# A column order and an operand place of its own for each Strassen tile (f32 attention and gated feed-forward, one core)

## The chip, the cores and the metric

The kernel runs on one core of a Trainium2 chip. The metric is the time of one execution on the device in microseconds (us). A core has TensorE for matrix products (PE in the profile; PEld is its loading of weights), VectorE (DVE), ScalarE (ACT), GpSimd (POOL), and SyncE (SP), which here issues all DMAs. SBUF is the on-chip memory, 128 partitions wide; PSUM holds the results of products. In a matmul one operand, the weights, is loaded into TensorE first, and the columns of the other, the moving operand, run through it.

## The reference

```python
def _attn_ref(q, k, v, g_norm):                       # 8 batches, 8 heads, 576 tokens, 64
    kv = np.einsum('bhsd,bhse->bhde', k, v)
    out = np.einsum('bhsd,bhde->bhse', q, kv)
    rms = np.sqrt(np.mean(out * out, axis=-1, keepdims=True) + 1e-06)
    return out / rms * g_norm

def _moe_ref(x, w_in, w_out):                         # x 4608 x 512, w_in 512 x 2048, w_out 2048 x 512
    h = x @ w_in
    g = h * (1.0 / (1.0 + np.exp(-h)))
    return g @ w_out
```

The output of the attention, with the heads of a token side by side, is the x of the second function. All is f32.

## The kernel before

**Precision.** Each f32 operand of the large products is split into an upper part that TensorE's faster f32 format (fp32r) holds exactly and a lower part, the rest. One product becomes three matmuls: upper by lower, lower by upper, upper by upper.

**Tiles.** The 4608 tokens are nine tiles of 512, t = 0 to 8. Tiles 0 and 1 form h = x @ w_in plainly: for each of the 16 blocks of 128 hidden units, `products` (line 470) issues 12 matmuls of 512 columns (line 474). Tiles 2 to 8 are the Strassen tiles: w_in and x are cut into quarters, and seven half-sized products on sums of quarters replace eight. Their sums of w_in are made during tile 1 (`make_sums`), sent to DRAM and loaded again for each step.

**A pair step** (`pair_step`, line 649) does a lower and an upper block of a Strassen tile, i = 0 to 7. It issues the products 1, 2, 6, 7, then 4, 5, 3, six matmuls each (`product`, line 628): 42 matmuls of 256 columns on line 634, whose weights are parts of w_in and whose moving operand is one of x's seven operands. Between them stand the projections of earlier blocks (`project`, line 499; line 505): gated h as weights, a block of w_out moving, 512 columns, three matmuls for each of four groups of 128 tokens and each of two blocks, 24 in a step. In the last tile one of the four groups is done in two halves of 256 columns. VectorE and ScalarE combine the products and apply the gate. The attention of later batches (lines 253 to 318) is spread over the steps of tiles 2 to 6 by a plan written out by hand; each engine runs its queue in the order of the code.

**x's operands.** `make_operand` (line 622) splits one of the seven sums of x into upper (ACT, line 625) and lower (DVE, line 626) parts of 256 columns by two row blocks: 4096 bytes a partition. This happens once a tile: `prepare` in the last step of the tile before makes 1, 2, 6, 7 when those products have been issued, and 4, 5, 3 after theirs. The dictionary `seven` gives each product its home j: 0 to 3 are inside x_place, the tile that held x of tile 1 (`x_second`), 4 to 6 in tiles tagged spare0 to spare2, which earlier held x of tile 0 and the sums of w_in.

**Places.** In the program before, x_place begins at byte 5344 of a partition, that is 224 modulo 256. Its homes begin SHIFT = 48 elements (192 bytes) later, at 160 modulo 256; so do spare0 to spare2. All blocks of w_in and w_out, the gates and q, k, v begin at 224 modulo 256. The inner offsets of the large operands are multiples of 512 bytes, so each matmul's operand begins at its tile's place modulo 256. The weights kh of the attention begin at 128, kl at 192.

Of the kernel before, what the change touches and what calls it, by code (L numbers as in the profile page):

```python
# [8 lines left out]
F32 = mybir.dt.float32  # L9
F32R = mybir.dt.float32r  # L10
# [20 lines left out]
def linear_attention_rms_silu_ffn(  # L31
# [22 lines left out]
    nc = tc.nc  # L54
    B, NP, P, S = q.shape
    D = P // 2
    DM = NP * P
    NF = w_in.shape[0]
    TN = 512
# [5 lines left out]
    const = ctx.enter_context(tc.tile_pool(name="const", bufs=1))  # L65
# [13 lines left out]
        nc.gpsimd.memset(t, 0.0)  # L79
    ident = const.tile([P, P], F32, name="ident", tag="kh", bufs=2)  # L80
    make_identity(nc, ident)
    warm_up = const.tile([P, 1], F32, name="warm_up")
    nc.gpsimd.memset(warm_up, 1.0)
    gcol = const.tile([P, 1], F32, name="gcol")
    both = const.tile([P, P], F32, name="both", tag="kl", bufs=2)
    nc.gpsimd.tensor_copy(out=both, in_=ident)
    for i in range(4):
        nc.gpsimd.tensor_copy(
            out=both[32 * i:32 * i + 32, 32 * (i ^ 1):32 * (i ^ 1) + 32], in_=ident[32 * i:32 * i + 32, 32 * i:32 * i + 32]
        )  # L90
    d_eps = const.tile([P, 1], F32, name="d_eps")
    nc.gpsimd.memset(d_eps, float(D) * EPS)

    def load_g():
        for h in range(P // D):
            nc.sync.dma_start(out=gcol[h * D:(h + 1) * D, :], in_=g_norm.rearrange("(d o) -> d o", o=1))
# [7 lines left out]

    SHIFT = 48
    x_place = const.tile([P, NP * 2 * TN + SHIFT], F32R, name="x_place")
    x_second = x_place[:, :NP * 2 * TN].rearrange("p (c a n) -> p c a n", c=NP, a=2)
    x_operands = x_place[:, SHIFT:].rearrange("p (c a k n) -> p c a k n", c=NP, a=2, k=2)  # L110
    x_first, lates = {}, {}

    def spare(n, shape, dtype, name):
        return const.tile(shape, dtype, name=name, tag=f"spare{n}")

    def late(n, shape, dtype, name):
        if not lates:
            const.tile([P, 64 - SHIFT], F32, name="gap")
        if name not in lates:
            lates[name] = const.tile(shape, dtype, name=name, tag=f"late{n}")  # L120
        return lates[name]
# [79 lines left out]
    def x_part(t, a, c):  # L201

        if t == 1:
            return x_second[:, c, a]
        if c not in x_first:
            kind = {"shape": [P, 2, TN], "dtype": F32R, "name": f"x{c}"}
            x_first[c] = spare(c, **kind) if c < 3 else late(0, **kind)
        return x_first[c][:, a]

    def segments(b):  # L210
# [288 lines left out]
    def project(t, f, gh, gl, bank, n, cs):  # L499
        first, last = order(t)[0], order(t)[-1]  # L500
        w = parts["wo", f]
        ns = slice(n * P, (n + 1) * P)
        bank = bank[:, :cs.stop - cs.start]
        for i, (g, a) in enumerate(((gh, 1), (gh, 0), (gl, 0))):
            nc.tensor.matmul(  # L505
                out=bank, lhsT=g[:, ns], rhs=w[:, a, cs], start=(f == first and i == 0), stop=(f == last and i == 2)
            )
# [8 lines left out]
    HF, H = NF // 2, TN // 2  # L516
    low, high = slice(0, H), slice(H, TN)
    sums_in_dram = dram.tile([HF, 2, P, 2, 2 * H], F32, name="sums_in_dram")
    operands, x_sums, once = {}, {}, {}

    def order(t):

        if t < 2:
            return [(f + t * HF) % NF for f in range(NF)]
        return [f for i in range(HF) for f in (i + HF, i)]

    def make_sums(i):

        lower, upper = (tmp.tile([P, S], F32, name=name, tag="tmp")[:, :TN] for name in ("lower", "upper"))
        sums = spare(0, [P, 4, H], F32, "sums")  # L530

        def whole(to, f):
            w = parts["wi", f].bitcast(F32)
            nc.vector.tensor_tensor(out=to, in0=w[:, 0, :], in1=w[:, 1, :], op=ALU.add)

        def combine(j, x, y, op=ALU.subtract):
            nc.vector.tensor_tensor(out=sums[:, j], in0=x, in1=y, op=op)

        def split(half):
            two = sums[:, 2 * half:2 * half + 2].rearrange("p j n -> p (j n)")  # L540
            both_parts = spare(1 + half, [P, 2, 2 * H], F32R, "sum_parts")
# [16 lines left out]

# [19 lines left out]
    def quarter(row, w):  # L578
        return late(row, [P, 2, TN], F32, f"x32_{row}")[:, :, w]
# [12 lines left out]
            )  # L592
        ]

    def operand(j):

        if j < 4:
            return x_operands[:, j]
        if j not in operands:
            operands[j] = spare(j - 4, [P, 2, 2, H], F32R, f"operand{j}")  # L600
        return operands[j]


    def of_block(half):
        return lambda i, a, c: parts["wi", i][:, a, half * H + c * P:half * H + (c + 1) * P]
# [6 lines left out]
    def of_sum(j):  # L612
        return lambda i, a, c: once[f"sums{j // 2}"][:, a, j % 2, c * P:(c + 1) * P]

    seven = {
        1: (4, lambda: quarter(0, low), of_block(0)), 2: (5, lambda: quarter(1, low), of_block(1)),
        6: (6, lambda: x_sums[2], of_sum(0)), 7: (1, lambda: x_sums[3], of_sum(1)),
        4: (0, lambda: x_sums[4], of_a22), 5: (2, lambda: x_sums[1], of_sum(2)),
        3: (3, lambda: quarter(1, high), of_sum(3)),
    }  # L620

    def make_operand(m):
        j, x, _ = seven[m]
        upper, lower = operand(j)[:, 0], operand(j)[:, 1]
        nc.scalar.copy(out=upper, in_=x())
        nc.vector.tensor_tensor(out=lower, in0=x(), in1=upper.bitcast(F32), op=ALU.subtract)

    def product(m, i, out):
        j, _, a_of = seven[m]
        x = operand(j)  # L630
        n = 0
        for c in range(2):
            for a, b in ((0, 1), (1, 0), (0, 0)):
                nc.tensor.matmul(  # L634
                    out=out, lhsT=a_of(i, a, c), rhs=x[:, b, c], start=(n == 0), stop=(n == 5)
                )
                n += 1

# [10 lines left out]
    def pair_step(t, i, groups):  # L649


        g = t * NF + 2 * i
# [11 lines left out]
        def prepare(*ms):  # L664

            for m in ms if fresh else ():
                make_operand(m)

        begin(g)
        bank, other = h_bank(), h_bank()  # L670
        u, v = bank[:, :H], bank[:, H:]
        y, z = other[:, :H], other[:, H:]
# [5 lines left out]
        u3 = p1  # L678
        if g == 2 * NF:
            due(4)  # L680
        product(1, i, u)
        product(2, i, v)
        product(6, i, y)
        product(7, i, z)
# [6 lines left out]
        if later:  # L691
            load_sums(i + 1, 0)
        prepare(1, 2, 6, 7)
        run(mid_jobs.pop(g, ()))
        product(4, i, u)
        product(5, i, v)
        product(3, i, y)
# [105 lines left out]
    with tc.manual_schedule():  # L803

        first = [FirstPair(c) for c in range(NP)]
        stats = at_bank().rearrange("p (c i j) -> p c i j", i=2, j=8)
        second = plan(1, 3)
        for item in ORDER.split():
            kind, n = item.rstrip("0123456789"), int(item.lstrip("wiopbg") or 0)
# [143 lines left out]
        at(last_jobs, NF + 13, lambda: make_operand(1))  # L953
        at(first_jobs, NF + 14, lambda: make_operand(2))
        at(mid_jobs, NF + 14, lambda: make_operand(6))
        for t in range(2, NT):
            spread_out(sums_of_x, 3 * (t * NF - 3), 1, 1, 1, 1)

# [1 line left out]
        for t in range(NT):  # L960
            sums = sums_of(t)
# [6 lines left out]
            for step, f in enumerate(order(t)):  # L968
                g = t * NF + step
# [27 lines left out]
                    job()  # L997
            if t == 1:
                for m in (7, 4, 5, 3):
                    make_operand(m)  # L1000
        lower_part(*late_part.pop())
        for old in sums:
            for item, _ in pend:
# [42 lines left out]
```

## Time and profile before

| what | value |
|---|---|
| two runs, median | 839.2 us (839.04 and 839.36) |
| the profiled execution, time | 839.63 us |
| its span, first to last instruction | 837.8 us |
| granted TensorE clock | 1.0 |
| TensorE matmuls | 5454 |
| products on line 634 | 2352 of 256 columns |
| projections on line 505 | 1680 of 512 columns, 96 of 256 |
| products on line 474 | 384 of 512 columns |
| waits of ACT for the first product of a step (line 685) | 140.9 us, TensorE being the one waited for |

The tiles by the start of their first Strassen product: tile 2 at 222.2 us, 3 at 308.7, 4 at 398.0, 5 at 487.3, 6 at 576.6, 7 at 663.0, 8 at 746.1. Tiles 2 to 6 hold attention work, tiles 7 and 8 hardly any.

How to read it: a matmul's busy time in the profile runs from its start until its result is out and overlaps the next one's; what counts for the total is the distance between starts. The profile's chain of waits gives pieces in order of time, each with its start, its length up to the next piece, the engine and line, and how many instructions it merges. Shapes such as 128x256 are partitions by columns.

### The profile page before, as it was taken

How to read it: one execution, taken by the hardware profiler on the slowest of the kernel's cores; microseconds unless marked ns; L12 is line 12 of the kernel's file. 1: busy time of each engine (PE TensorE's matmuls, PEld its weight loads, DVE VectorE, ACT ScalarE, POOL GpSimd, SP SyncE). 2: the span in 40 equal slices, each digit the busy share in tenths (PEclk: the TensorE clock that was granted, in tenths of full speed). 3: DMA queues.
4: the chain of work that ended last, by engine and by line, in shares of the span. 5: the costliest groups of instructions: out<-in, count | busy, mean ns of one | idle time of the engine just before them, and what ended most of it. 6: DMA issues, size and time to landing. Idle time of an engine off the chain costs nothing.

```text
span 837.8 us, 14032 instructions
## 1 busy us (share of the span) xinstructions
PE 826.8 (99%) x5454; PEld 734.6 (88%) x5454; DVE 528.9 (63%) x1027; ACT 359.0 (43%) x744; POOL 145.9 (17%) x142
## 2 busy tenths in 40 slices
PE   8999999999999999999999999999999999999998
PEld 7767888888899999998999998999999999999997
DVE  4886875788476567657766667656865664464332
ACT  3766564534453245325532355225532432243222
POOL 2786983423010002000200011001100000000000
PEclk9999999999999999999999999999999999999999
DMA  8879011337343634364424452444423343334331
GB/s 322 313 257 362 4 57 51 136 145 261 122 161 100 215 115 146 101 214 144 165 91 160 163 173 88 158 158 157 151 84 103 106 155 103 105 102 151 100 102 51
DMA packets 42418, 122.55 MB, mean 146 GB/s; under 512 B 4848, under 2 KB 5104, under 8 KB 42352
## 3 DMA queue, kind: packets, MB, share of 16 engines
q1 hardware_dynamic: 42352, 121.65, 42.4%
q8 instruction: 43, 0.70, 0.4%
q14 instruction: 23, 0.19, 0.1%
HBM read 103.81 MB, written 17.83 MB: 145 GB/s over the span
## 4 chain that ended last, share of the span: by engine, by line
PE 94%; DMA 4%; POOL 1%; ACT 0%; issue 0%; SPq 0%
PE acc L505 46%; PE hp L634 33%; PE hp L474 9%; PE at L253 2%; DMA k<-in_k 1%; DMA wo<-in_moe_w_out 1%; DMA early_wi<-in_v 1%; DMA v<-in_v 1%; PE at L289 1%; PE at L288 1%; PE at L290 1%; PE at L505 1%; DMA wi<-in_moe_w_in 1%; PE at L286 1%; POOL wo L191 0%
## 5 line engine op out<-in xcount | busy, mean ns | idle before, releaser
L505 PE MATMUL acc<-wo,gh 128*128 128x512 f32 (+1 forms) x1152 | 354.1, 389 | 0.1
L505 PEld LDWEIGHTS acc<-wo,gh 128*128 128x128 f32 x1152 | 210.3, 188 | 39.7 <-POOL wo L191 0.3
L505 PE MATMUL acc<-wo,gl 128*128 128x512 f32 x576 | 223.0, 387 | 0.5 <-POOL gl L485 0.5
L634 PE MATMUL hp<-x_place,wi 128*128 128x256 f32 x1344 | 167.8, 280 | 0.0
L634 PEld LDWEIGHTS hp<-x_place,wi 128*128 128x128 f32 x1344 | 162.0, 189 | 0.0
L634 PEld LDWEIGHTS hp<-operand,wi 128*128 128x128 f32 x1008 | 126.0, 189 | 3.9
L505 PEld LDWEIGHTS acc<-wo,gl 128*128 128x128 f32 x576 | 108.1, 188 | 23.5 <-POOL gl L485 0.9
L634 PE MATMUL hp<-operand,wi 128*128 128x256 f32 x1008 | 127.5, 281 | 0.0
L275 POOL TENSOR_TENSOR ql<-q,qh 128x576 fp32r<-128x576 f32 x24 | 35.6, 1483 | 376.0 <-ACT qh L274 341.9
L685 ACT COPY wi<-hp 128x256 f32<-128x256 f32 x56 | 20.9, 373 | 140.9 <-PE hp L634 140.9
L643 ACT ACTIVATE gh<-gf 128x512 fp32r<-128x512 f32 x56 | 35.4, 633 | 94.4 <-DVE gf L698 81.6
L643 ACT ACTIVATE gh<-wi 128x512 fp32r<-128x512 f32 x56 | 35.5, 634 | 79.8 <-DVE wi L698 68.0
L686 DVE TENSOR_TENSOR gf<-hp,wi 128x256 f32<-128x256 f32 x28 | 11.9, 425 | 84.8 <-ACT wi L685 84.8
L686 DVE TENSOR_TENSOR wi<-hp,wi 128x256 f32<-128x256 f32 x28 | 11.9, 424 | 84.3 <-ACT wi L685 84.3
L474 PE MATMUL hp<-x,wi 128*128 128x512 f32 x180 | 46.4, 402 | 1.4 <-POOL wi L191 1.4
L474 PE MATMUL hp<-x_place,wi 128*128 128x512 f32 x192 | 46.4, 390 | 0.0
L647 DVE TENSOR_TENSOR gl<-wi,gh 128x512 fp32r<-128x512 f32 x56 | 38.4, 685 | 11.4 <-ACT wi L644 11.4
L687 DVE TENSOR_TENSOR wi<-hp,wi 128x256 f32<-128x256 f32 x56 | 23.8, 425 | 32.3 <-PE hp L634 32.3
L647 DVE TENSOR_TENSOR gl<-gf,gh 128x512 fp32r<-128x512 f32 x56 | 39.0, 696 | 7.3 <-ACT gf L644 7.3
L294 ACT ACTIVATE sq<-at 128x288 f32<-128x288 f32 x56 | 22.9, 410 | 45.6 <-PE at L290 38.9
L474 PEld LDWEIGHTS hp<-x_place,wi 128*128 128x128 f32 x192 | 35.7, 188 | 7.3
L316 DVE SCALAR_TENSOR_TENSOR x<-o,gcol,yT 128x128 f32<-128x128 f32 (+7 forms) x52 | 40.7, 784 | 1.9
(142 smaller groups left out, 1006.8 us busy)
## 6 DMA issues: line engine op xcount, KB each, us to landing
wi<-sums_in_dram SPq DMA_DIRECT2D x112, 512.0 KB, 3.3
out<-ob SPq DMA_DIRECT2D x35, 256.0 KB, 2.4
wi<-in_moe_w_in SPq DMA_DIRECT2D x16, 512.0 KB, 7.8
wo<-in_moe_w_out SPq DMA_DIRECT2D x16, 512.0 KB, 8.9
sums_in_dram<-sum_parts SPq DMA_DIRECT2D x16, 512.0 KB, 2.6
k<-in_k SPq DMA_DIRECT2D x28, 288.0 KB, 5.2
v<-in_v SPq DMA_DIRECT2D x28, 288.0 KB, 5.4
q<-in_q SPq DMA_DIRECT2D x28, 288.0 KB, 4.0
```

Source lines behind the costliest of these rows:

```text
L253: nc.tensor.matmul(out=self.kv[h], lhsT=self.k[rows, c, :], rhs=self.v[rows, c, :], start=(start and r == 0), stop=(stop and r == 4),)
L275: nc.gpsimd.tensor_tensor(out=self.ql, in0=self.q, in1=self.qh.bitcast(F32), op=ALU.subtract)
L294: nc.scalar.activation(out=self.sq[:, self.w], in_=self.ps, func=AF.Square)
L316: nc.vector.scalar_tensor_tensor(out=to, in0=self.o[:, a:e], scalar=gcol, in1=self.yT, op0=ALU.mult, op1=ALU.mult)
L474: nc.tensor.matmul(out=hp[:, :TN], lhsT=w[:, a, fs], rhs=x_part(t, b, c), start=(c == 0 and i == 0), stop=(c == NP - 1 and i == 2),)
L505: nc.tensor.matmul(out=bank, lhsT=g[:, ns], rhs=w[:, a, cs], start=(f == first and i == 0), stop=(f == last and i == 2))
L634: nc.tensor.matmul(out=out, lhsT=a_of(i, a, c), rhs=x[:, b, c], start=(n == 0), stop=(n == 5))
L643: nc.scalar.activation(out=gh, in_=x, func=AF.Silu)
L647: nc.vector.tensor_tensor(out=gl, in0=x, in1=gh.bitcast(F32), op=ALU.subtract)
L685: nc.scalar.copy(out=p1, in_=u)
L686: nc.vector.tensor_tensor(out=c1[:, low], in0=v, in1=p1, op=ALU.add)
L687: nc.vector.tensor_tensor(out=u2, in0=y, in1=p1, op=ALU.add)
```

## The change

In the Strassen tiles 2 to 8 the columns of a matmul's moving operand and of its output are taken in an order given by the tile, the same for both, so that each result lands where it did. "On" is the old order. "Back" takes runs of 16 columns from the last to the first. "Woven" takes a run of 16 from the lower half, one from the upper half, and so on; "woven back" does that from the end. This holds for the seven products and for the tile's projections. Tiles 0 and 1 stay as they were.

Each Strassen tile also has a shift of 0, 16, 32 or 48 elements (0 to 192 bytes), which never falls from one tile to the next. The five operands in x_place and spare0 begin that much behind the start of their home; x_place and spare0 are longer by 64 elements for it. The operands in spare1 and spare2 are not shifted. Products 7, 4, 5, 3 get the homes 3, 2, 1, 0 in the order in which they are made. The homes in the spares are new tiles of the pool for each t.

The small tiles ahead of x_place are put in another order and a gap of 8 elements is added. Counted from the sizes, x_place then begins at byte 5376, spare0 at 22016 and the blocks of weights at 42752, all 0 modulo 256; what follows moves by 288 bytes. The memset of warm_up on POOL, and with it ACT's first use of it, comes after the five copies that make `both`.

```diff
-    warm_up = const.tile([P, 1], F32, name="warm_up")
-    nc.gpsimd.memset(warm_up, 1.0)
-    gcol = const.tile([P, 1], F32, name="gcol")
     both = const.tile([P, P], F32, name="both", tag="kl", bufs=2)
     nc.gpsimd.tensor_copy(out=both, in_=ident)
...
+    warm_up = const.tile([P, 1], F32, name="warm_up")
+    nc.gpsimd.memset(warm_up, 1.0)
+    gcol = const.tile([P, 1], F32, name="gcol")
     d_eps = const.tile([P, 1], F32, name="d_eps")
     nc.gpsimd.memset(d_eps, float(D) * EPS)
+    const.tile([P, 8], F32, name="gap")
...
-    SHIFT = 48
-    x_place = const.tile([P, NP * 2 * TN + SHIFT], F32R, name="x_place")
+    WAYS = {
+        2: ("woven", 0), 3: ("back", 0), 4: ("woven back", 16), 5: ("woven", 16), 6: ("woven", 32),
+        7: ("woven back", 48), 8: ("on", 48),
+    }
+    SLACK = 48
+    x_place = const.tile([P, NP * 2 * TN + 64], F32R, name="x_place")
     x_second = x_place[:, :NP * 2 * TN].rearrange("p (c a n) -> p c a n", c=NP, a=2)
-    x_operands = x_place[:, SHIFT:].rearrange("p (c a k n) -> p c a k n", c=NP, a=2, k=2)
...
-    def spare(n, shape, dtype, name):
-        return const.tile(shape, dtype, name=name, tag=f"spare{n}")
+    def spare(n, dtype, name, shift=0):
+        size = 2 * TN + 64 * (n == 0)
+        full = const.tile([P, size], dtype, name=name, tag=f"spare{n}")
+        return full[:, shift:shift + 2 * TN]
 
     def late(n, shape, dtype, name):
-        if not lates:
-            const.tile([P, 64 - SHIFT], F32, name="gap")
...
             nc.tensor.matmul(
-                out=bank, lhsT=g[:, ns], rhs=w[:, a, cs], start=(f == first and i == 0), stop=(f == last and i == 2)
+                out=moved(t, bank), lhsT=g[:, ns], rhs=moved(t, w[:, a, cs]), start=(f == first and i == 0), stop=(f == last and i == 2)
             )
...
-    def operand(j):
-
+    def operand(j, t):
+
+        shift = WAYS[t][1]
         if j < 4:
-            return x_operands[:, j]
-        if j not in operands:
-            operands[j] = spare(j - 4, [P, 2, 2, H], F32R, f"operand{j}")
-        return operands[j]
+            at = j * 2 * TN + shift
+            return x_place[:, at:at + 2 * TN].rearrange("p (a k n) -> p a k n", a=2, k=2)
+        if (j, t) not in operands:
+            operands[j, t] = spare(j - 4, F32R, f"operand{j}", shift * (j == 4)).rearrange("p (a k n) -> p a k n", a=2, k=2)
+        return operands[j, t]
+
+    def moved(t, ap):
+
+        way = WAYS.get(t, ("on",))[0]
+        if way == "on":
+            return ap
+        if way == "back":
+            return ap.rearrange("p (k e) -> p k e", e=16)[:, ::-1]
+        ap = ap.rearrange("p (h k e) -> p k h e", h=2, e=16)
+        return ap if way == "woven" else ap[:, ::-1]
...
-        6: (6, lambda: x_sums[2], of_sum(0)), 7: (1, lambda: x_sums[3], of_sum(1)),
-        4: (0, lambda: x_sums[4], of_a22), 5: (2, lambda: x_sums[1], of_sum(2)),
-        3: (3, lambda: quarter(1, high), of_sum(3)),
+        6: (6, lambda: x_sums[2], of_sum(0)), 7: (3, lambda: x_sums[3], of_sum(1)),
+        4: (2, lambda: x_sums[4], of_a22), 5: (1, lambda: x_sums[1], of_sum(2)),
+        3: (0, lambda: quarter(1, high), of_sum(3)),
     }
...
                 nc.tensor.matmul(
-                    out=out, lhsT=a_of(i, a, c), rhs=x[:, b, c], start=(n == 0), stop=(n == 5)
+                    out=moved(t, out), lhsT=a_of(i, a, c), rhs=moved(t, x[:, b, c]), start=(n == 0), stop=(n == 5)
                 )
...
-                make_operand(m)
+                make_operand(m, t + 1)
```

The other edits pass t to `make_operand`, `product` and `operand`, and give the earlier users of the spare tiles their old shapes.

More of the change, by code (lines that the diff above doesn't have):

```diff
@@ L206, in x_part @@
             kind = {"shape": [P, 2, TN], "dtype": F32R, "name": f"x{c}"}
-            x_first[c] = spare(c, **kind) if c < 3 else late(0, **kind)
+            x_first[c] = spare(c, F32R, f"x{c}").rearrange("p (a n) -> p a n", a=2) if c < 3 else late(0, **kind)
         return x_first[c][:, a]
@@ L529, in make_sums @@
         lower, upper = (tmp.tile([P, S], F32, name=name, tag="tmp")[:, :TN] for name in ("lower", "upper"))
-        sums = spare(0, [P, 4, H], F32, "sums")
+        sums = spare(0, F32, "sums").rearrange("p (j n) -> p j n", n=H)
         def whole(to, f):
@@ L540, in split @@
             two = sums[:, 2 * half:2 * half + 2].rearrange("p j n -> p (j n)")
-            both_parts = spare(1 + half, [P, 2, 2 * H], F32R, "sum_parts")
+            both_parts = spare(1 + half, F32R, "sum_parts").rearrange("p (a n) -> p a n", a=2)
             nc.scalar.copy(out=both_parts[:, 0], in_=two)
@@ L616, in linear_attention_rms_silu_ffn, with make_operand, product @@
         1: (4, lambda: quarter(0, low), of_block(0)), 2: (5, lambda: quarter(1, low), of_block(1)),
-        6: (6, lambda: x_sums[2], of_sum(0)), 7: (1, lambda: x_sums[3], of_sum(1)),
-        4: (0, lambda: x_sums[4], of_a22), 5: (2, lambda: x_sums[1], of_sum(2)),
-        3: (3, lambda: quarter(1, high), of_sum(3)),
+        6: (6, lambda: x_sums[2], of_sum(0)), 7: (3, lambda: x_sums[3], of_sum(1)),
+        4: (2, lambda: x_sums[4], of_a22), 5: (1, lambda: x_sums[1], of_sum(2)),
+        3: (0, lambda: quarter(1, high), of_sum(3)),
     }
-    def make_operand(m):
+    def make_operand(m, t):
         j, x, _ = seven[m]
-        upper, lower = operand(j)[:, 0], operand(j)[:, 1]
+        upper, lower = operand(j, t)[:, 0], operand(j, t)[:, 1]
         nc.scalar.copy(out=upper, in_=x())
         nc.vector.tensor_tensor(out=lower, in0=x(), in1=upper.bitcast(F32), op=ALU.subtract)
-    def product(m, i, out):
+    def product(m, t, i, out):
         j, _, a_of = seven[m]
-        x = operand(j)
+        x = operand(j, t)
         n = 0
@@ L680, in pair_step @@
             due(4)
[L681 to L684, printed above, removed]
+        product(1, t, i, u)
+        product(2, t, i, v)
+        product(6, t, i, y)
+        product(7, t, i, z)
         nc.scalar.copy(out=p1, in_=u)
@@ L694, in pair_step @@
         run(mid_jobs.pop(g, ()))
-        product(4, i, u)
-        product(5, i, v)
-        product(3, i, y)
+        product(4, t, i, u)
+        product(5, t, i, v)
+        product(3, t, i, y)
         nc.vector.tensor_tensor(
@@ L952, in linear_attention_rms_silu_ffn @@
         at(last_jobs, NF + 13, lambda: load_sums(0, 0, 1))
-        at(last_jobs, NF + 13, lambda: make_operand(1))
-        at(first_jobs, NF + 14, lambda: make_operand(2))
-        at(mid_jobs, NF + 14, lambda: make_operand(6))
+        at(last_jobs, NF + 13, lambda: make_operand(1, 2))
+        at(first_jobs, NF + 14, lambda: make_operand(2, 2))
+        at(mid_jobs, NF + 14, lambda: make_operand(6, 2))
         for t in range(2, NT):
@@ L999, in linear_attention_rms_silu_ffn @@
                 for m in (7, 4, 5, 3):
-                    make_operand(m)
+                    make_operand(m, 2)
         lower_part(*late_part.pop())
```

## The prediction

> **What bounds the kernel now.** I read the page's engine shares first, then the list of whom TensorE waited for, then the chain of waits in the Strassen tiles.
>
> ```profile
> PE 826.8 (99%) x5454; PEld 734.6 (88%) x5454; DVE 528.9 (63%) x1027; ACT 359.0 (43%) x744; POOL 145.9 (17%) x142
> PE 94%; DMA 4%; POOL 1%; ACT 0%; issue 0%; SPq 0%
> ```
> ```profile
> PE hp L824 <- POOL ident masks.py:199: 2.0, 1, 2.0
> PE hp L474 <- POOL wi L191: 1.4, 1, 1.4
> ...
> PE acc L505 <- POOL gl L485: 0.5, 1, 0.5
> ```
>
> The first line is busy time (us), the second the chain that ended last; the other fence has the first two and the last of the seven rows that say whom TensorE waited for (us in total, times, longest). TensorE is the bound, and no product of line 634 is in that list: from tile 2 on TensorE waits for nobody. So the time there is the number of matmuls times the distance from one start to the next, and only this distance can change. Busy times of matmuls overlap, so I take distances from the chain, where a piece ends where the next begins. A pair step of tile 7, one of tile 8, and blocks of tiles 0 and 1:
>
> ```profile
> 688.88 5.44 PE acc L505 x24
> 694.33 4.95 PE hp L634 x42
> ...
> 782.23 2.41 PE acc L505 x12
> 784.64 0.36 PE at L505 x3
> 785.00 2.42 PE acc L505 x12
> 787.42 0.36 PE at L505 x3
> 787.78 4.78 PE hp L634 x42
> ```
> ```profile
> 101.28 2.79 PE hp L474 x12
> ...
> 189.52 2.72 PE hp L474 x12
> ```
>
> In tile 7 the 42 products of 256 columns stand 4.95/42 = 117.9 ns apart and the 24 projections of 512 columns 5.44/24 = 226.7 ns. In tile 8 the same 42 products, from the same addresses, by the same instructions, stand 4.78/42 = 113.8 ns apart. 226.7/2 = 113.3, so tile 8 is at the price per column of the projections, 226.7/512 = 0.443 ns, and tiles 2 to 7 pay 4 to 5 ns a product on top of it. No engine is waited for in either, so I read these 4 ns as two reads in each other's way: the moving operand and the weights that are loaded at the same time (TensorE's weight loads are busy 88%). Where the operands begin matters too. In tile 1 x and w_in both begin at 224 modulo 256 bytes: 2.72/12 = 226.7 ns. In tile 0 three of the four x blocks begin 64 bytes lower: 2.79/12 = 232.5 ns. And the projections of half width in tile 8 (both operands at 224) stand 0.36/3 = 120.0 ns apart. So 113.3, 117.9 and 120.0 ns are three states of one stream, and which one it falls into depends on place and on what came before. By tile, the products of line 634 alone (busy us, count):
>
> ```profile
> 308.72:398.02 89.30, 41.08 (x337) 40.78 (x337) 1.00 0.45 147
> 398.02:487.31 89.29, 41.08 (x337) 40.78 (x336) 1.00 0.44 146
> 487.31:576.60 89.29, 41.08 (x336) 40.78 (x336) 1.00 0.45 147
> 576.60:663.00 86.40, 41.08 (x336) 40.78 (x336) 1.00 0.34 114
> 663.00:746.10 83.10, 40.88 (x337) 40.72 (x337) 1.00 0.35 115
> 746.10:837.80 91.70, 39.86 (x336) 39.16 (x335) 1.00 0.31 104
> ```
>
> Tiles 3 to 6 agree to 0.01 us: the state is no accident but repeats. The granted clock is 1.00 throughout.
>
> **The change part by part.** It adds no matmul, copy, DMA or wait that the code names. Its parts:
>
> *Column order in the products of tiles 2 to 7.* 6 tiles x 8 steps x 42 = 2016 products. "Woven" takes 16 columns of the lower half, then 16 of the upper: both lie in the same 64 bytes modulo 256, so the read stays twice as long in each quarter of 256 bytes. At 113.3 ns for 256 columns a quarter then lasts 2 x 16 x 0.443 = 14.2 ns; a weight load of 128 columns spread over the same 113.3 ns also takes 14.2 ns a quarter. The two would walk in step, and x's place decides how far apart. If that works, a step goes from 4.95 to 4.78: 0.17 us, 1.36 us a tile. For the woven tiles 2, 5 and 6 I take all of it: -4.1 us. "Woven back" (4 and 7) stays as long in a quarter but walks against the weights; I take half, -1.4 us. "Back" (3) only walks against them; I take nothing. The bounds: all six tiles at 4.78, 48 x 0.17 = -8.2 us; all six in the 120.0 ns state, 42 x 0.120 = 5.04 instead of 4.95, 48 x 0.09 = +4.3 us.
>
> *Column order in the projections of tiles 2 to 7.* 48 x 24 = 1152 matmuls of 512 columns. They are already at the lowest distance that the rows show, and nothing there can be won but little in the steps with attention work. The nearest row of a worse state is tile 0's 232.5 ns: +5.8 ns x 1152 = +6.7 us. Their two operands begin at the same place before and after, so I take zero, and keep +6.7 for the range.
>
> *Places.* All that stands behind x_place moves by 288 bytes, so weights, x and gates begin at 0 instead of 224 modulo 256, and in tile 0 x now begins where w_in begins. That is tile 1's case: 2.72 instead of 2.79, 16 blocks, at most -1.1 us. Early blocks wait for data, so I take -0.5. In the attention products the moving side goes from 224 to 0, one weight side from 192 to 128:
>
> ```profile
> 232.81 0.13 PE at L288
> 232.94 0.14 PE at L289
> 233.07 0.13 PE at L290
> ```
>
> These vary between 0.13 and 0.14 us; 144 of them by 0.01 is 1.4 us at most, either sign. I take zero.
>
> *Operands made anew for each tile.* The seven ACT copies and seven DVE subtractions a tile stay. The new homes are ordered from the highest (product 7 in the fourth) downwards and the shift never falls from tile to tile, so the part of a home that overlaps its neighbour's old one has been read by then. The tightest place is the start of tile 2:
>
> ```profile
> 219.43 0.63 ACT L625 CAST x_place<-x 128x512 fp32r<-128x512 f32 x1
> 220.45 0.68 DVE L626 TENSOR_TENSOR x_place<-x,x_place 128x512 fp32r<-128x512 f32 x1
> 224.27 1.93 PE L634 MATMUL hp<-x_place,wi 128*128 128x256 f32 x15
> ```
>
> The last operand is ready at 220.45 + 0.68 = 221.1 and the first product that reads x_place starts at 224.3: 3.1 us of cover. Tile 1's last block reads x's fourth part 9 matmuls after its first, 2.0 us later, and product 7 now goes there first; that still fits, and costs nothing. Without the cover each copy would show with 0.6 to 0.7 us, once. The warm-up memset on POOL goes behind five copies:
>
> ```profile
> 2.03 0.20 ACT L828 ACTIVATE warm_up<-warm_up 128x1 f32<-128x1 f32 x1
> 2.31 0.94 POOL L88 COPY both<-ident 32x32 f32<-32x32 f32 x4
> 7.63 0.43 ACT L261 COPY kvm<-hp 64x64 f32<-64x64 f32 x2 [5.40 <-PE hp L253]
> ```
>
> ACT's warm-up then starts at about 3.3 instead of 2.03, and ACT idles until 7.63 anyway: zero.
>
> *Sum:* -4.1 - 1.4 - 0.5 = -6.0 us. The profiled execution took 839.6 us (its span is 837.8), the median of the two runs 839.2; against the median that is 833.2 us.
>
> [...] The rows say that the same product costs 113.8 or 117.9 ns while weights load beside it. [...]
>
> **The rivals.**
>
> 1. *All is won.* All six tiles reach 4.78 (-8.2), tile 0 gains in full (-1.1), and steps with attention work a little (about -1): 829 us. For it: tile 8 shows that state at 782 to 792 us and holds it. Against it: six different settings would all have to be good.
>
> 2. *Nothing moves.* The state is set by what precedes the products, not by order: 839 us, with tile 0's gain 838. For it: same addresses, two states (tile 7 and tile 8).
>
> 3. *The new orders fall into worse states.* Products at 120.0 ns (+4.3) and projections at 232.5 (+6.7): up to 850 us; half of it is 845. For it: the woven tile 2 and all projections start both streams in the same quarter, where the half-width projections stand at 120.0; walking backwards meets the weights more often. It decides against the change once the projections lose over 5 ns each.
>
> 4. *Slower by a mechanism of its own: a jump costs a column.* Every 16 columns the address now jumps, in x or w_out and in the accumulator's bank. Jumps: 2016 x 16 + 1152 x 32 = 69,120. If each costs one column's time, 0.443 ns, that is +30.6 us: 870 us. It decides from 17/30.6 = 0.55 of a column on, where the loss passes 2% with nothing won. For it: no row shows a matmul with a broken run. Against it: runs of 16 are long. [...]
>
> 5. *The column itself becomes cheaper.* A plain f32 product of 288 columns stands as two records:
>
> ```profile
> 50.97 0.48 PE at L286 x2
> ...
> 58.06 0.48 PE at L286 x2
> ```
>
> That is 0.48/2/288 = 0.833 ns a column and record, a little under two of today's 0.443. If it is two steps a column, a step is 0.417 ns. If the missing 0.026 ns is a stumble from one 64 bytes to the next that a woven order avoids, 69,120 x 16 columns x 0.026 = -28.8 us: 810 us. Against it: every 512-column row, at either place, is at 0.443 or more.
>
> **How the numbers follow.** Forecast (partial gain, 831 to 836) 0.32; all won 0.15; nothing moves 0.12; worse states (840 to 852) 0.22; jumps cost 0.12; cheaper columns 0.07. The predicted time is the forecast's, 833.2 us. The range 826 to 852 leaves out the last two, 0.19: its low end is rival 1 with attention products gaining 1.4 and 1 us of rounding in the rows, its high end rival 3 with the attention products losing. About 2% (17 us) is what a measurement of this kernel can surely tell from no change: faster by that only if columns get cheaper, 0.07; slower only if jumps cost, 0.12; within 0.81.
>
> **What would show it.** In the chain of waits the steps of tiles 2, 5 and 6 should read about 4.78 for 42 products, tile 3 4.95, tiles 4 and 7 between; the 24 projections 5.44 everywhere; tile 8 as now; tile 0's blocks of 12 about 2.72. Steps over 5.04, or projections over 5.6, speak for rival 3; both up in proportion to their columns, by more than 2% in all of tiles 2 to 7 and not in tile 8, for rival 4; under 4.7 and 5.4, for rival 5. A wait of TensorE on ACT or DVE at a tile's start would show that the homes do collide, which I have at zero.

## The result and the profile after

The changed kernel takes 851.9 us (851.8 to 851.95), the kernel before 839.2: a ratio of 1.015, 95% interval 1.011 to 1.020. It is slower, by 12.7 us or 1.5%, clear of the noise. The profiled execution has a span of 850.0 us instead of 837.8.

TensorE is still the bound, and waits as little as before. The list of whom it waited for, in the changed kernel (the first two and the last of six rows; us in total, times, longest):

```profile
PE hp L844 <- POOL ident masks.py:199: 1.9, 1, 1.9
PE hp L482 <- POOL wi L199: 1.5, 1, 1.5
...
PE acc L513 <- POOL gl L493: 0.5, 1, 0.5
```

Again no Strassen product (line 654) is in it, so none of their operands was late: the cost lies in the distances between matmuls. The chain of waits of the changed kernel has them (start, length, line, count). Line 482 is what was line 474, the products of tiles 0 and 1; line 654 the Strassen products (634 before); line 513 the projections (505 before). One pair step each of tiles 2 to 7, and two blocks of tile 0 first:

```profile
100.29 2.72 PE hp L482 x12
...
105.73 2.72 PE hp L482 x12
```
```profile
253.67 5.04 PE hp L654 x42
258.71 5.76 PE acc L513 x24
...
345.50 4.95 PE hp L654 x42
350.45 5.60 PE acc L513 x24
```
```profile
435.75 4.92 PE hp L654 x42
440.67 5.54 PE acc L513 x24
...
526.28 5.05 PE hp L654 x42
531.33 5.76 PE acc L513 x24
...
618.85 5.12 PE hp L654 x42
623.97 5.76 PE acc L513 x24
...
715.59 4.98 PE hp L654 x42
720.57 5.60 PE acc L513 x24
```

Before, every steady step of these tiles had 4.95 and 5.44. The 24 projections now take 5.76 us where the order is woven (tiles 2, 5, 6: 240 ns apart), 5.60 where it is back (tile 3) or woven back (7), 5.54 in tile 4. The 42 products are between 4.92 and 5.12. Adding up, over tiles 2 to 7, the distances from each matmul's start to the next one's:

| us | before | changed |
|---|---|---|
| tiles 0 and 1, from their first matmul | 220.2 | 219.0 |
| products of tiles 2 to 7 (2016) | 237.2 | 240.6 |
| projections in tiles 2 to 7 (1140) | 260.3 | 269.9 |
| tile 8, to the end | 88.5 | 89.0 |

So +3.4 from the products, +9.6 from the projections, +0.5 from the last tile, -1.2 at the start: 12.3 us in all, and with the attention products 0.1 us shorter the 12.2 us by which the span grew. Four fifths of it is in the projections; that this is their order of columns, the experiments below show.

### The profile page after: what moved, and what is told of

Same layout as the page of the kernel before. It is cut to its first block, busy times and chain, and to the rows that moved or that the text cites. A ratio compares the mean times of both kernels' runs of the same rounds, so it can differ in the third digit from the quotient of the medians.

```text
span 850.0 us, 14031 instructions
## 1 busy us (share of the span) xinstructions
PE 839.9 (99%) x5454; PEld 740.4 (87%) x5454; DVE 529.3 (62%) x1027; ACT 359.6 (42%) x744; POOL 145.7 (17%) x142
## 4 chain that ended last, share of the span: by engine, by line
PE 94%; DMA 4%; POOL 1%; ACT 0%; issue 0%; SPq 0%
PE acc L513 46%; PE hp L654 33%; PE hp L482 9%; PE at L261 2%; DMA wo<-in_moe_w_out 1%; DMA k<-in_k 1%; DMA v<-in_v 1%; PE at L296 1%; PE at L298 1%; PE at L297 1%; DMA wi<-in_moe_w_in 1%; PE at L513 1%; DMA early_wi<-in_v 1%; PE at L294 1%; POOL wo L199 0%
## 5 line engine op out<-in xcount | busy, mean ns | idle before, releaser
L513 PE MATMUL acc<-wo,gh 128*128 128x512 f32 (+1 forms) x1152 | 360.7, 395 | 0.1
L513 PE MATMUL acc<-wo,gl 128*128 128x512 f32 x576 | 226.7, 394 | 0.5 <-POOL gl L493 0.5
L654 PE MATMUL hp<-x_place,wi 128*128 128x256 f32 x1344 | 169.8, 281 | 0.0
L654 PEld LDWEIGHTS hp<-x_place,wi 128*128 128x128 f32 x1344 | 163.9, 189 | 0.0
L482 PEld LDWEIGHTS hp<-x_place,wi 128*128 128x128 f32 x192 | 35.8, 188 | 7.3
```

Source lines behind the costliest of these rows:

```text
L482: nc.tensor.matmul(out=hp[:, :TN], lhsT=w[:, a, fs], rhs=x_part(t, b, c), start=(c == 0 and i == 0), stop=(c == NP - 1 and i == 2),)
L513: nc.tensor.matmul(out=moved(t, bank), lhsT=g[:, ns], rhs=moved(t, w[:, a, cs]), start=(f == first and i == 0), stop=(f == last and i == 2))
L654: nc.tensor.matmul(out=moved(t, out), lhsT=a_of(i, a, c), rhs=moved(t, x[:, b, c]), start=(n == 0), stop=(n == 5))
```

## The experiments

At the start there were two theories of mine; no trace shows either at work. J (jumps): each jump from one run of 16 columns to another costs the moving operand's read some time, wherever it jumps to. M (meeting): the moving read and the read of the next weights meet in a quarter of 256 bytes, and what counts is place and pace of the two. Each kernel is a variant of the changed one unless something else is said; the tiles hold different settings side by side. In all variants of it but the first, the products are "on" at shift 48 in every tile. Ratios are to the kernel before, run beside them (839.15 to 839.35 us). A kernel given as "one execution" is read by its steps alone. The diffs show the main lines, without the ends of long ones. The tables below give one steady step, read from the chain of waits, as 24 projections or 42 products.

**Places alone.** All orders "on", x's shift still differing from tile to tile.

```diff
-        2: ("woven", 0), 3: ("back", 0), 4: ("woven back", 16), 5: ("woven", 16), 6: ("woven", 32),
-        7: ("woven back", 48), 8: ("on", 48),
+        2: ("on", 0), 3: ("on", 0), 4: ("on", 16), 5: ("on", 16), 6: ("on", 32), 7: ("on", 32), 8: ("on", 48),
```

> All orders are 'on', the places of the changed kernel stay, with x's shift 0, 0, 16, 16, 32, 32, 48 for tiles 2 to 8. Theory J (each jump in a column order costs time, places cost little): projections of tiles 2 to 7 at 226.7 ns apart in the steps without attention, products 113 to 118 ns, about 838 us in all. Theory M (the moving read and the weight read meet, and place decides how often): projections 226.7 too, since both of their operands begin alike, but the products differ from shift to shift, 120 ns at shift 0 as in the half-width projections of the last tile, about 842 us.

Measured: 843.2 us, ratio 1.005 (1.003 to 1.006). The shifts of tiles 2 to 6 are those of the changed kernel; tile 7 has 32 instead of 48. Its chain of waits in tiles 2, 4 and 6 (line 653 products, 512 projections):

```profile
258.08 5.47 PE acc L512 x24
263.55 5.03 PE hp L653 x42
...
438.19 5.48 PE acc L512 x24
443.67 4.98 PE hp L653 x42
...
617.93 5.49 PE acc L512 x24
623.42 5.01 PE hp L653 x42
```

The projections are back near 5.44. The products cost as much as in the changed kernel: summed over tiles 2 to 7, 240.7 us against its 240.6. In tiles 2 to 6, where the shifts are the same, it is 200.7 in both, against 197.6 before. So the loss there comes from x's places, and the orders, taken together, neither won nor lost. By tile they did: the changed kernel's products take 0.65 and 0.5 us less than the straight ones in tiles 3 (back) and 4 (woven back), 0.1, 0.5 and 0.6 us more in the woven tiles 2, 5 and 6. That the place counts speaks for M in the products.

**Orders in the projections alone**, products "on" at shift 48 in all tiles.

```diff
-                out=moved(t, bank), lhsT=g[:, ns], rhs=moved(t, w[:, a, cs]),
+                out=moved(t, bank, ORDERS), lhsT=g[:, ns], rhs=moved(t, w[:, a, cs], ORDERS),
```

> Orders in the projections alone (woven, back, woven back, woven, woven, woven back for tiles 2 to 7), products 'on' at shift 48. J and M both: projections as in the changed kernel, 240 ns woven, 232 to 235 ns in the two backward orders. Products: 118 ns if what precedes them does not matter; if a state is carried over from the projections, other values than before, between 113 and 120. About 839 + 1152 x 10 ns = 850 us, so that nearly the whole loss is here.

Measured: 845.6 us, one execution. A step of tile 2 (woven) and of tile 7 (woven back), line 654 products, 513 projections:

```profile
268.53 5.76 PE acc L513 x24
274.28 4.88 PE hp L654 x42
...
709.86 4.88 PE hp L654 x42
714.74 5.60 PE acc L513 x24
```

The projections come out as in the changed kernel, but for tile 4 (5.60 instead of 5.54); they sum to 270.1 us, against 260.6 us with all orders "on" (the kernel further down). The products stand at 4.85 to 4.88 in all tiles, better than the 4.95 before. So the total is under the 850 us that I had written: the places were worth 6.0 us in straight products, from 240.7 in the kernel with places alone to 234.7 with all orders "on" at shift 48 (234.4 here). Woven back at shift 48, tile 7 of the changed kernel, takes 39.9 us for the tile's products; straight at that shift takes 39.0.

**The length of the runs.** Projections woven in tiles 2 to 7, in runs of 4 to 128.

```diff
+    RUNS = {2: 4, 3: 8, 4: 16, 5: 32, 6: 64, 7: 128}
...
-        ap = ap.rearrange("p (h k e) -> p k h e", h=2, e=16)
+        ap = ap.rearrange("p (h k e) -> p k h e", h=2, e=e)
```

> Projections woven in all of tiles 2 to 7, with runs of 4, 8, 16, 32, 64 and 128 columns instead of 16; products 'on' at shift 48. J, one clock of 0.42 ns a jump: 280, 253, 240, 233, 230 and 228 ns for 512 columns. M: no smooth fall with the run; runs of 4 and 8 stay as long in a quarter of 256 bytes as runs of 16 and cost the same 240, the longer ones come out in steps of about 6.7 ns (226.7, 233.3 or 240).

Measured (847.0 us, one execution), 24 projections on line 514, tiles 2 to 7 in turn:

```profile
258.64 6.03 PE acc L514 x24
...
351.32 5.84 PE acc L514 x24
...
442.81 5.76 PE acc L514 x24
...
533.73 5.67 PE acc L514 x24
...
623.83 5.46 PE acc L514 x24
...
706.50 5.45 PE acc L514 x24
```

That is 251, 243, 240, 236, 227.5 and 227 ns. Both theories miss. J's 0.42 ns a jump is what the woven projections of the changed kernel lose, (240 - 226.7) / 32; that it is one clock no run shows. Its 280 and 253 for the short runs are too high, and its 230 for runs of 64 too; M had short runs at 240. What stands out is that runs of 64 and more, which are whole turns of 256 bytes, cost nothing although they jump: straight projections at these places take 5.46 us too (the kernel with all orders "on").

**One side alone.** The order is taken by the read or by the write; the columns of h w_out then come out permuted.

```diff
-                out=moved(t, bank), lhsT=g[:, ns], rhs=moved(t, w[:, a, cs]),
+                out=moved(t, bank, WRITTEN), lhsT=g[:, ns], rhs=moved(t, w[:, a, cs], READ),
```

> In the projections the order is taken by one side only: read in the order and written straight in tiles 2 (woven), 4 (back), 6 (woven back); read straight and written in the order in tiles 3, 5, 7 (the columns of h w_out then come out permuted). Products 'on' at shift 48. If the read in SBUF costs (M, and J of the read): 240, 235, 232 ns in tiles 2, 4, 6 and 226.7 in 3, 5, 7. If the write in PSUM costs (J of the write): 226.7 in 2, 4, 6 and 240, 235, 232 in 3, 5, 7. If each side costs a jump of its own, both in between.

Measured (840.1 us, one execution), line 514: tile 2 (read woven), 4 (read back), 5 (written back), 6 (read woven back) and 7 (written woven back):

```profile
268.29 5.76 PE acc L514 x24
...
447.85 5.60 PE acc L514 x24
...
537.38 5.46 PE acc L514 x24
...
615.99 5.60 PE acc L514 x24
...
699.54 5.46 PE acc L514 x24
```

With tile 3 (written woven) at 5.46 too, the whole cost is in the read from SBUF. The order of the write into PSUM, in runs of 16, costs nothing.

**Which quarter follows which.** A third theory, Q: what counts is the turn in which the moving read takes the quarters of 256 bytes. Here the projections of tiles 2 to 7 read w_out from the start of its upper part, in given patterns, so the output is another sum. In tiles 2 and 7 the pattern reaches column 767 and so runs on into the lower part behind it.

```diff
+    PATTERNS = {
+        2: [[64, 4], [80, 8], [1, 16]], 3: [[16, 16], [256, 2], [1, 16]], 4: [[16, 4], [64, 8], [1, 16]],
+        5: [[64, 8], [16, 4], [1, 16]], 6: [[16, 2], [32, 16], [1, 16]], 7: [[64, 4], [80, 8], [1, 16]],
+    }
...
+        flat = w[:, 0, :]
+        return bass.AP(tensor=flat.tensor, offset=flat.offset, ap=[list(flat.ap[0])] + PATTERNS[t])
```

> The projections of tiles 2 to 7 read w_out's upper part alone, in fixed patterns of 16-column runs (written straight; the output is then another sum). Tiles 2 and 7: each run 80 columns after the last, a jump at every run, but the quarters of 256 bytes in the straight turn 0, 1, 2, 3. Tile 3: woven, each quarter twice. Tile 4: each quarter for eight runs. Tile 5: the straight order, only written down in runs. Tile 6: quarters 0, 2, 0, 2, then 1, 3, 1, 3. Products 'on' at shift 48. If a jump costs (J): 240 ns in tiles 2, 3, 4, 6, 7 and 226.7 in 5. If the turn of the quarters counts (Q): 226.7 in 2, 5 and 7, 240 in 3, more than 240 in 4, about 233 in 6.

Measured (842.5 us, one execution), line 512, tiles 2 to 7 in turn:

```profile
278.21 5.46 PE acc L512 x24
...
357.45 5.76 PE acc L512 x24
...
448.38 5.74 PE acc L512 x24
...
538.61 5.46 PE acc L512 x24
...
628.19 5.75 PE acc L512 x24
...
712.32 5.45 PE acc L512 x24
```

J falls for runs of 16: in tiles 2 and 7 the address jumps at every run, and nothing is lost while the quarters come in their straight turn. Out of turn costs 0.30 us for 24, 12.5 ns a projection, and much the same for each quarter twice, for eight times, or for 0, 2, 0, 2. Q had the direction right but not the size: more than 240 in tile 4 and 233 in tile 6 did not come. Nor does Q cover the shortest runs: woven in runs of 4 or 8 takes the quarters in the same turn as in runs of 16 and yet cost 251 and 243 ns.

**The place of the weights.** The gates begin 64 or 128 bytes later modulo 256: a tile of 16 or 32 f32 elements is put ahead of them. The projections are woven in tile 2, back in 4, woven back in 6 and "on" elsewhere.

```diff
+    ahead = ctx.enter_context(tc.tile_pool(name="ahead", bufs=1))
+    ahead.tile([P, 16], F32, name="ahead")
     gp = ctx.enter_context(tc.tile_pool(name="gp", bufs=LAG + 1))
```

> The gates, which are the weights of the projections, begin 64 bytes later modulo 256; w_out as before. Projections woven in tile 2, back in 4, woven back in 6, 'on' in 3, 5, 7, 8; products 'on' at shift 48. If the moving read meets the weight read (M): 'on' no longer 226.7 but about 232.5, as in tile 0 of the kernel before, where the two operands lie 64 bytes apart, and woven another value than 240. If the moving read pays for its own order alone: 226.7 'on', 240 woven, 233 back, as with gates and w_out at one place.

> As with 64 bytes, but the gates 128 bytes later. M: 'on' and woven at values that differ both from those at one place and from those at 64 bytes, in steps of about 6.7 ns. The moving read alone: 226.7, 240, 233 once more.

| 24 projections, us | gates with w_out | 64 bytes later | 128 bytes later |
|---|---|---|---|
| on | 5.46 | 5.59 | 5.58 |
| woven | 5.76 | 5.76 | 5.76 |
| back | 5.60 | 5.65 | 5.67 |
| woven back | 5.60 | 5.46 | 5.48 |

The two kernels took 845.1 and 844.0 us, one execution each. The rows of the second column, in the order of the tiles 2 (woven), 3 (on), 4 (back) and 6 (woven back), line 515:

```profile
271.11 5.76 PE acc L515 x24
...
372.23 5.59 PE acc L515 x24
...
451.63 5.65 PE acc L515 x24
...
630.91 5.46 PE acc L515 x24
```

The moving operand, its order and its place are the same in all three columns. So the straight order and woven back do feel where the weights lie, as M says; woven does not, and back hardly.

**Fewer weights.** If the meeting of reads is the cost, a shorter weight load must cost less. The projections between a tile's first and last block load only some of the columns of the gates, and leave out the other rows of the output.

```diff
+            m = P if f in (first, last) else NARROW.get(t, P)
...
-                out=moved(t, bank), lhsT=g[:, ns], rhs=moved(t, w[:, a, cs]),
+                out=moved(t, bank[:m], ORDERS), lhsT=g[:, n * P:n * P + m], rhs=moved(t, w[:, a, cs], ORDERS),
```

> In the projections of tiles 2 to 7, all but those of the first and last block load fewer columns of the gates as weights (32 in tiles 2, 3, 4; 64 in 5 and 7; 96 in 6) and so leave out the other rows of the output; the moving columns are the same 512. Orders: woven in 2, 5, 6, back in 4, 'on' in 3 and 7. Products 'on' at shift 48. If the loss comes from meeting the weight read (M), it shrinks with the load: woven 230 ns at 32 columns, 233 at 64, 237 at 96, back 229 at 32, 'on' 226.7. If the moving read pays for its order without any weights (I): woven 240 at all widths, back 233, 'on' 226.7.

> Projections woven back in tiles 2 to 5 and 'on' in 6 and 7; weights of 128 columns in tiles 2 and 7, 32 in 3, 64 in 4, 96 in 5 and 6 (first and last block of a tile always 128; the other rows of the output are left out). Products 'on' at shift 48, gates and w_out at one place. Woven back depended on the place of the gates (5.59 us for 24 at one place, 5.46 and 5.48 with the gates 64 and 128 bytes later), so if meeting the weight read is its cost, it shrinks with the load: 5.59 in tile 2, about 5.56 in 5, 5.52 in 4, 5.47 in 3. If the width does not matter, as it did not for woven: 5.59 in all four. 'On' with 96 columns: 5.46 if the width does not matter, 5.5 or more as with 32 and 64 columns if what counts is when in the moving read the load falls.

| 24 projections, us | 128 columns | 96 | 64 | 32 |
|---|---|---|---|---|
| woven | 5.76 | 5.76 | 5.76 | 5.76 |
| back | 5.60 | | | 5.60 |
| woven back | 5.60 | 5.48 | 5.52 | 5.48 |
| on | 5.46 | 5.52 | 5.52 | 5.55 |

The two kernels took 844.4 and 837.4 us, one execution each. From the first kernel tile 2 (woven, 32 columns) and tile 3 (on, 32), from the second tile 2 (woven back, 128) and tile 3 (woven back, 32), line 515 in both:

```profile
258.00 5.76 PE acc L515 x24
...
348.61 5.55 PE acc L515 x24
```
```profile
257.65 5.60 PE acc L515 x24
...
347.23 5.48 PE acc L515 x24
```

For woven M falls: a quarter of the load costs the same 5.76. For woven back a shorter load does cost less, but not in proportion: 96 columns, expected at 5.56, cost as little as 32, and 64 cost more than either. "On" gets worse with a shorter load, so what counts there is not how much is read beside it; that it is when the load falls is argued, not shown.

**All orders on, all shifts 48.**

```diff
-        2: ("woven", 0), 3: ("back", 0), 4: ("woven back", 16), 5: ("woven", 16), 6: ("woven", 32),
-        7: ("woven back", 48), 8: ("on", 48),
+        2: ("on", 48), 3: ("on", 48), 4: ("on", 48), 5: ("on", 48), 6: ("on", 48), 7: ("on", 48), 8: ("on", 48),
```

> The changed kernel with every order 'on' and every shift 48. From the tiles seen so far: tiles 0 and 1 218.8 us instead of 220.2, products 116.2 instead of 117.7 ns (tiles 2 to 7, -3.0 us), projections as before or 0.5 us worse, the last tile +0.4: 835.5 us, 0.5% faster than before. If the gain of tiles 0 and 1 is lost later, 837.

Measured: 836.6 us, ratio 0.997 (0.996 to 0.998), 1 us above what was written. A step of tile 7, line 653 products, 512 projections:

```profile
691.34 4.88 PE hp L653 x42
696.22 5.46 PE acc L512 x24
```

This kernel shows how the products' states arise. Its products in another step of tile 7, by operand (records' shortest, median and longest in ns):

```profile
L653 PE MATMUL hp<-x_place,wi x24: 276/276/286, 714.0 to 716.6; 128*128 128x256 f32 x24
L653 PE MATMUL hp<-operand,wi x18: 278/283/283, 711.8 to 713.9; 128*128 128x256 f32 x18
```

Product 1, the first six, stands 117.8 ns apart, as in tile 7 of the kernel before. Products 2 and 6, whose operands lie in spare1 and spare2, are not shifted by the change and begin where their weights begin: 120.0 ns, records of 283 ns. And the 24 products from x_place, which come after those, need 120 or 121, 121 or 122 and 116 ns once and then 113.4, records of 276 ns. With the same shift of 48 elements product 1, which comes after the projections, stays at 117.8. The kernel before has both on the same addresses: in tile 7 all 42 products of a step stand 117 to 119 ns apart, in tile 8, after three projections of half width, 120, 122 and 116 ns once and then 113 or 114. So this stream, 64 bytes apart, has two states that both last, and here what ran before it chose.

**Halves ahead of the products.** That suggested an edit to the kernel before: let the last group of projections ahead of the products run in halves of 256 columns, as its last tile does.

```diff
+        halves = [slice(0, cs.stop - cs.start)]
+        if t >= 2 and f < HF and n == TN // P - 1 and cs.stop - cs.start == DM:
+            halves = [slice(0, DM // 2), slice(DM // 2, DM)]
+        for half in halves:
+            for i, (g, a) in enumerate(((gh, 1), (gh, 0), (gl, 0))):
+                nc.tensor.matmul(
+                    out=bank[:, half], lhsT=g[:, ns], rhs=w[:, a, cs.start + half.start:cs.start + half.stop],
+                    start=(f == first and i == 0), stop=(f == last and i == 2 and half is halves[-1])
+                )
```

> The kernel before, with one edit: in tiles 2 to 7 the last group of projections ahead of the products is issued as two times three matmuls of 256 columns instead of three of 512, as the last tile of the kernel before does with one group. If the state of the products is carried over from what precedes them (S), they fall into the last tile's state: 42 in 4.78 us instead of 4.95 in all of tiles 2 to 7, the halves cost 0.04 us a step more, 48 x -0.13 = -6.2 us, 833 us. If the state belongs to the tile and not to what precedes: products stay at 4.95, 841 us.

Measured: 833.8 us, ratio 0.993 (0.992 to 0.995). A step of tile 7, line 639 products, 509 projections (21 of 512 columns and 6 of 256):

```profile
693.83 5.49 PE acc L509 x27
699.32 4.78 PE hp L639 x42
```

The products fall from 4.95 to 4.78, the projections rise from 5.44 to 5.49, as expected. This beats both kernels by adding three matmuls to a step. It is the test of the reading above: here, what runs just before the products sets their state.

**Halves, and x of tile 0 beside w_in.** To the kernel before with halves, one more edit: two of the parts of tile 0's x begin 16 elements later, where w_in begins modulo 256.

```diff
+        at, size = 16 * (n < 2 and name[0] == "x"), math.prod(shape[1:])
+        full = const.tile([P, size + 64 * (n < 2)], dtype, name=name, tag=f"spare{n}")[:, at:at + size]
```

> As the kernel with halves, and x of tile 0 begins where w_in begins in two more of its four parts (spare0 and spare1 start x 16 elements later). S and M: 833 us less two thirds of the 1.2 us that tiles 0 and 1 gained in the changed kernel, 832 us; tile 0's blocks of 12 products 2.75 us instead of 2.79.

Measured: 833.4 us, ratio 0.993 (0.992 to 0.994). Tile 0's blocks of 12 are at 2.75 as expected, and the products on that line sum to 91.5 us instead of 91.9 in the kernel with halves alone. The total moved by the same 0.4 us, which the intervals do not tell from nothing; 832 was expected.

## Why the prediction was wrong, by its own steps

*What bounds the kernel* held: no new wait, no operand late, and the distance between matmuls is all that changed. Operands made anew and the later warm-up cost nothing, as written.

*Column order in the projections* is the step that failed. It took zero, because moving operand and weights begin at the same place before and after. But the cost is in the order itself: 24 projections take 5.76 instead of 5.44 us in the woven tiles, and the sum is +9.6 us. The upper bound of +6.7 us, from tile 0's 232.5 ns, was too low as well: no row of the profile before showed a broken order, and the worst row of a straight one did not bound it. What counts, in runs of 16, is the turn in which the read from SBUF takes the quarters: a jump at every run in the straight turn costs nothing (5.46 us).

*Column order in the products* took -5.5 us from an idea of mine, that a woven read walks in step with the weights and x's place sets the gap. Measured was 5.04 to 5.12 us a step in the woven tiles instead of 4.78, at all three places, and in tiles 5 and 6 woven is worse than straight at the same place. In the projections woven does not feel where or how many weights are loaded (5.76 us at three places and at four widths), so the walk in step has no support. That a weight load spends 14.2 ns in each quarter, and in which order it takes them, was my assumption; no run shows it. Over tiles 2 to 7 the products lost 3.4 us: about 2.5 by x's places (each tile's straight products at its shift, summed from the two kernels with orders "on") and 0.9 by the orders. I had also not drawn the consequence that products 2 and 6 stay unshifted: they start at their weights' place, which the prediction itself had as the 120.0 ns state. In tile 8, forecast "as now", this makes most steps 4.86 instead of 4.78.

*Places* came out as bounded for tile 0; x's places in the products had no term of their own. In tile 0 the blocks of 12 read 2.72 as forecast, worth 0.7 us on that line (91.9 to 91.2 us in all); the other 0.5 us at the start lies ahead of them, where the kernel before waited 1.0 us for a load in its first attention products and the changed one does not. The kernel with halves alone, whose code for tiles 0 and 1 is that of the kernel before, is 0.8 us shorter there too, so this part is no effect of the change. The attention products became 0.1 us shorter.

*The rivals.* The second had its mechanism right and its outcome wrong: what precedes the products does choose their state, as the kernel with halves shows (4.95 to 4.78 us), but places and orders moved them too. The third, worse states, is what happened, with its condition met: projections lose over 5 ns each. It had 0.22. Its price, 11.0 us, was 1.7 us short, and its parts were off: 9.6 instead of 6.7 from the projections, 3.4 instead of 4.3 from the products. That the measured time lies just under the end of the range, 852, is therefore partly luck. Where it said that projections suffer from both streams starting in one quarter, it was wrong, since the straight order is best there (5.46 us, against 5.59 and 5.58 with the gates elsewhere). That walking backwards meets the weights more often no run shows, only what it costs: 5.60 instead of 5.46 us in runs of 16. The fourth, a jump that costs a column, is refuted, for runs of 16, by the pattern that jumps at each run in the straight turn and loses nothing (5.46 us). Nor do jumps in the accumulator's bank cost anything in runs of 16: written out of order, 24 projections take 5.46 us, as in order.

The prediction's reading, that the moving read and the weight load are in each other's way, has this for it: with the moving side untouched, moving the weights by 64 bytes takes 24 straight projections from 5.46 to 5.59 us. Against it, the woven ones stay at 5.76.

*Open.* Why the woven read costs 0.3 us whatever the weights do, while woven back, which also takes each quarter twice, can run without loss (5.46 us with the gates 64 bytes later). Why runs of 4 and 8 cost more than runs of 16. Whether the two reads meet, and what they do then, was not seen, only what place and order cost: 5.46 to 5.76 us.

## What to carry to other kernels

Where matmuls stand back to back, read the distance between their starts, not their durations, and compare equal ones across stages: a difference without a wait was a state here, and what ran just before chose it (4.95 or 4.78 us for the same 42 products). Let a moving operand be read straight through, or at least in whole turns of 256 bytes (5.46 us for 24 projections either way, 5.76 woven in runs of 16); the order of the write, in runs of 16 columns, cost nothing here (5.46 us). Shift operands against their weights only when each setting has been measured, since no setting's value carried over to the next: 42 straight products took 5.03, 4.98, 5.01 and 4.88 us at shifts of 0, 16, 32 and 48 elements.

## What the runs showed of the hardware

- A moving operand in fp32r costs 0.443 ns a column in the best rows (226.7 ns for 512), and reading it in runs of 4, 8, 16 and 32 columns from two halves in turn costs 251, 243, 240 and 236 ns; in runs of 64 or 128, 227.
- In runs of 16 columns, what counted is the turn of the four 64-byte quarters of 256 bytes: 5.46 us for 24 projections in the straight turn with a jump at every run, 5.74 to 5.76 in three other turns, all with the gates and w_out at one place.
- One stream had two states that both lasted: 256 columns, with the operand 64 bytes from its weights, stood 117.8 or 113.4 ns apart. In the kernel before it was the first after projections of 512 columns (42 products in 4.95 us) and the second after three or, in the kernel with halves, six projections of 256 columns (4.78 us).
